# A written table in place of a build-time clock for the order of five engines' work

## The chip, the cores and the metric

The kernel runs on one core of one Trainium2 chip. The metric is the device time of one execution in microseconds (us). A core has five engines that each work through their own list of instructions in order and wait for one another by semaphores: TensorE (PE: matmuls, with weight loads, PEld, that overlap them), VectorE (DVE), ScalarE (ACT), GpSimd (POOL) and SyncE (SP), which here only starts transfers (DMAs). Matmuls write into PSUM, eight banks of 128 x 512 float32; everything else lies in SBUF, with 128 partitions.

## The reference

The input x has 2048 rows of 512 in bfloat16. Two attention layers and two feed-forward layers alternate, each on the layer norm of x and added to x, with the same weights both times:

```python
    x = A_x
    x = x + _A_ref(_layernorm(x, axis=-1), A_wq, A_wk, A_wv, A_wo, A_beta)
    x = x + _B_ref(_layernorm(x, axis=-1), B_w_gate, B_w_up, B_w_down)
    x = x + _A_ref(_layernorm(x, axis=-1), A_wq, A_wk, A_wv, A_wo, A_beta)
    x = x + _B_ref(_layernorm(x, axis=-1), B_w_gate, B_w_up, B_w_down)
```

`_B_ref` is `gelu(x @ w_gate) * (x @ w_up) @ w_down` with 1792 columns between. `_A_ref` is attention with a memory: 32 heads of 16, four segments of 512 rows that are worked through in order:

```python
            logits = jnp.einsum('bhqd,bhkd->bhqk', qs, ks) * scale + mask
            p = _softmax(logits, axis=-1)
            a_dot = jnp.einsum('bhqk,bhkd->bhqd', p, vs)
            pq = phi(qs)
            num = jnp.einsum('bhld,bhde->bhle', pq, M)
            den = jnp.einsum('bhld,bhd->bhl', pq, z)[..., None] + 1e-06
            a_mem = num / den
            o = g * a_mem + (1.0 - g) * a_dot
            outs.append(o)
            pk = phi(ks)
            M = M + jnp.einsum('bhld,bhle->bhde', pk, vs)
            z = z + jnp.einsum('bhld->bhd', pk)
```

Here `phi(t)` is t + 1 for positive t and exp(t) otherwise, and the mask leaves each query the keys up to its own place. The heads' results go through wo.

## The kernel before

x, all weights and one segment's intermediate results stay in SBUF. The work goes by segments of 512 rows: 8 for attention (4 in each of two layers) and 8 for the feed-forward layers, and work of neighbouring segments is mixed so that PE always has some.

**Attention, one segment.** Layer-norm statistics are taken on DVE; the normalised rows, xn, are written by DVE or POOL (L734), turned by a DMA or by PE (L425) into xnT, and multiplied with wq, wk and wv. Each product of 512 columns is four matmuls of 128 x 128 weights by 512 columns into a bank; the bank is copied ("evicted") by DVE (L601) or ACT (L602). kx holds two masked copies of k (L546, L551). Scores come in rounds: a visit of two rounds puts narrow matmuls of four row groups into four banks (`score`, L1670; "rows" mode: weights with 16 or 32 rows, four of them side by side in the array). ACT takes the exponential of a pair of banks at once (128 x 1024), or, where the four banks lie in a row, of all four (128 x 2048), into pt (L1710); POOL masks what lies on the diagonal (L1646, L1651), or DVE does (L1656). Value products multiply pt by the v of a segment (vaug, whose constant column gives the softmax sum, and vz for shared rounds) with four matmuls of 32 columns side by side ("columns" mode); DVE turns (L1209), scales (L1219) and turns back (L1232). phi is an exponential on ACT, a minimum with 1 on DVE or POOL (L989) and a max-and-add on DVE (L970). The memory's products give num and den, and its result is added to the heads' (L1235). Products with wo are added to x by DVE (L1287).

**Feed-forward, one segment.** 14 gate tiles (gelu on ACT), 14 up tiles (multiplied with the gate's on DVE, L1388), and 14 products to each of four blocks of rows by wd, added to x. wd_sb and gel_sb serve as buffers of the first segment until they are needed: rows of q and k of segment 0 lie in wd_sb.

**What sets the order.** `order` (L402) runs at build time. `Clocks` and four `Engine` objects hold a modelled time of each engine, with a cost per instruction. Work of the other engines is posted with a ready time and a slack, and each modelled engine takes the job with the least of them; evictions, masks, minima and xn may be posted to two engines, and whichever is free first by the model takes them. PE's work are items with a due time. The loop at the end of `order` asks at every step: are two score rounds ready and four banks free (`rounds_now`); is an item open; can one be opened in a free bank; and if nothing can, it issues a fill, a product of 128 columns on a tile of ones (`warm`), 24 times in all. Some 100 numbers in `POLICY`, with `CHANGES` per 20 us of modelled time, `NUDGES` and `VISITS`, weigh the choices. The model has a cost for changes of mode (`SWITCH`) and for instruction fetch (`sent`).

**Whole or columns.** The array takes a product as one matmul of 128 x 128 weights ("whole") or as four of 128 x 32 in columns mode, which is the mode of the value products. `product` (L605) decides by the mode PE is in, and by whether a value product is near:

```python
        if ck.mode == "columns" or ck.mode == "rows" and (any(it.kind == "flush" and it.near() for it in items)):
            ck.tiling("columns")
```

All of PE's matmuls go through `multiply` (L421).

Of the kernel before, what the change touches and what calls it, by code (L numbers as in the profile page):

```python
# [44 lines left out]
HALVED = ()  # L45
BOTH = (0, 1)
EARLY = [(1, 192, 64, 0), (0, 64, 192, 64)]
LATE = [([(3, 448, 64, 0), (2, 320, 192, 64)], 2), ([(0, 256, 256, 0)], 0), ([(1, 256, 256, 0)], 0)]


def shared(*tiles):
    return [(b, BOTH, ki, P * ki, C, C * n) for n, (b, ki) in enumerate(tiles)]


def whole_block(b):
    rounds = []
    for par in range(2):
        rounds += [([(b, (par,), *piece) for piece in pieces], n) for pieces, n in zip(FULL, DIAG)]
        if not par:
            rounds.append((shared(*((b, ki) for ki in range(TPS))), None))  # L60
    return rounds, ((0, 0, SHARED + 1), (1, SHARED, ROUNDS))


def table(halved):

    rounds, units = [], []

    def add(got):
        rounds.extend(got)
        return range(len(rounds) - len(got), len(rounds))  # L70

    def early(b):
        return [([(b, (par,), *piece) for piece in EARLY], 2) for par in range(2)]

    def late(b):
        return [([(b, (par,), *piece) for piece in pieces], n) for pieces, n in LATE for par in range(2)]

    for b in range(1 if halved else KT):
        got, parts = whole_block(b)
        at = add(got)  # L80
        units.append((b, None, [((par,), [at[i] for i in range(i0, i1)]) for par, i0, i1 in parts]))
    if halved:
        a1, s12, a2 = add(early(1)), add([(shared((1, 0), (1, 1), (2, 0), (2, 1)), None)]), add(early(2))
        a3, s3 = add(early(3)), add([(shared(*((3, ki) for ki in range(TPS))), None)])
        units += [(1, 0, [(BOTH, [*a1, *s12])]), (2, 0, [(BOTH, [*a2, *s12])]), (3, 0, [(BOTH, [*a3, *s3])])]
        units.append((3, 1, [(BOTH, [*s3, *add(late(3))])]))
        l1 = add(late(1))
        s12 = add([(shared((1, 2), (1, 3), (2, 2), (2, 3)), None)])
        units += [(1, 1, [(BOTH, [*l1, *s12])]), (2, 1, [(BOTH, [*s12, *add(late(2))])])]
    assert len(rounds) == STEPS  # L90
    flushes = [(u, b, h, n, pars, used) for u, (b, h, fl) in enumerate(units) for n, (pars, used) in enumerate(fl)]
    return rounds, len(units), flushes


TABLES = [table(k in HALVED) for k in range(NK)]
FLUSHES = [[[f for f in TABLES[k][2] if max(f[5]) == t] for t in range(STEPS)] for k in range(NK)]
USERS = [[sum(t in f[5] for f in TABLES[k][2]) for t in range(STEPS)] for k in range(NK)]
UNIT0 = [sum(TABLES[i][1] for i in range(k)) for k in range(NK)]
FLUSH0 = [sum(len(TABLES[i][2]) for i in range(k)) for k in range(NK)]


BY_PE = {("xnTf", 0), ("xnTf", 1), ("xnTf", NK - 1)}
QUICK = {("xnTf", k): (2,) for k in HALVED}
# [11 lines left out]
POLICY = dict(
    flush_wait=-12.009, piece_slack=-25.599, kb_slack=-71.296, mem_slack=-20.591, qk_due=-62.012, e_q=-288.808,
    e_k=138.109, exp_slack=-4.686, e_slack=148.266, phi_slack=52.68, gelu_slack=19.624, act_evict=2.071,
    first_evict=4.769, gate_step=1.835, up_due=3.98, up_step=-6.05, down_due=84.578, down_step=14.696, upd_due=9.144,  # L120
    kb_act=663.078, vz_slack=0.687, x_dve=-0.049, v0_due=-232.366, x1_at=-21.812, x2_at=-35.702, x3_at=1.468,
    x3_load=-242.902, direct=2, gelu_tiles=0, look=-61.488, lag=0, wv_at=-9.865, xn_pool=-26.108, kb_pool=62.128,
    cut_pool=0.028, at_pool=-27.695, gate_due=4.711, shun=77.466, col_gap=6.814, hold=34, early=435.185,
    starve=-5.581, near=-26.359, cap=6, soon=-134.054, drain=-0.14, join=0, held=10, urge_a1=-29.527, urge_a2=-0.64,
    urge_a3=-0.468, urge_a4=-5.519, urge_a5=-268.031, urge_a6=-6.935, urge_a7=-34.222, urge_f0=-37.767,
    urge_f1=-6.779, urge_f2=-11.706, urge_f3=-0.081, urge_f4=51.11, urge_f5=-14.712, urge_f6=-5.12, urge_f7=-38.117,
    half_a1=14, half_a4=21, half_a5=4, half_a6=18, half_a7=14, half_f0=21, half_f1=8, half_f2=10, half_f3=24,
    half_f4=46, half_f5=6, half_f6=8, pair_a1=10, pair_a2=3, pair_a3=12, pair_a4=11, pair_a5=0, pair_a6=65,
    pair_a7=28, pair_f0=9, pair_f1=19, pair_f2=43, pair_f3=2, pair_f4=22, pair_f5=23, pair_f6=28, pair_f7=11,
    turn_a1=14, turn_a2=12, turn_a3=8, turn_a4=8, turn_a5=6, turn_a6=16, turn_a7=42, turn_f2=18, turn_f3=4,  # L130
    turn_f4=16, turn_f5=2, turn_f6=6)

# [1723 lines left out]
```

## Time and profile before

| | |
|---|---|
| runs of the kernel, us | 539.11, 539.22, 541.04 (median 539.22) |
| span of the profiled execution, us | 539.1 |
| PE busy, us (instructions) | 521.3 (9,006 matmuls recorded) |
| weight loads, PEld | 274.5 (9,072) |
| DVE, ACT, POOL busy, us | 449.0, 433.2, 286.2 |
| bytes moved by DMA | 27.96 MB, mean 52 GB/s |

The profiled execution's own time is its span. Busy is time with at least one instruction under way; matmuls run in a pipeline, so their recorded durations overlap and the time from one start to the next is the price of one. A row of the groups gives line, engine, operation, out<-in, the shape, the count, then busy us, mean ns of one, and the idle time ahead of them with what ended it. A row of the windows gives a stretch, and busy us and instructions of PE, PEld, DVE, ACT and POOL in it, then PE's granted clock as a share of full speed, DMA share and GB/s. A row of the waits gives the waiting engine, tile and line, what it waited for, and total us, times and longest us. A row of the timeline gives start, duration, and in brackets the idle time ahead.

### The profile page before, as it was taken

Reading aid. Unit: us, or ns where it says so; the run is one execution under the profiler, and the core shown is the slowest. Engines: PE = TensorE matmul, PEld = TensorE weight load, DVE = VectorE, ACT = ScalarE, POOL = GpSimd, SP = SyncE. Lnnn points to the kernel's source line nnn. Section 1 sums busy time; section 2 is a strip of 40 time slices with the busy share of each in tenths; the row PEclk is TensorE's granted clock in tenths of the full one; section 3 lists DMA queues with packets and bytes.
Section 4 is the critical chain, followed back from the end, with each engine's and each line's share of the span. In section 5 each row is a group of like instructions: output and inputs, shape, how many; then the busy total and the mean of one; then the engine's idle time right before and its main releaser. Section 6 shows DMA issues by size and latency. Waiting matters only on the chain.

```text
span 539.1 us, 20839 instructions
## 1 busy us (share of the span) xinstructions
PE 521.3 (97%) x9006; PEld 274.5 (51%) x9072; DVE 449.0 (83%) x849; ACT 433.2 (80%) x559; POOL 286.2 (53%) x360
## 2 busy tenths in 40 slices
PE   8999999999999999999999999999989999999997
PEld 4444467446654454554544454454554456555444
DVE  7998897899999997898997999878988786786342
ACT  6999997998999978999899778889789968830320
POOL 4997853279778656647572387550655253301000
PEclk9999999999999999999999999999999999999999
DMA  8349302422011123311432120310121004100001
GB/s 270 85 109 208 93 19 54 128 41 62 13 32 41 24 46 49 52 33 21 52 80 32 23 43 12 71 35 9 33 71 24 0 16 98 14 2 30 11 0 40
DMA packets 69134, 27.96 MB, mean 52 GB/s; under 512 B 53426, under 2 KB 69042, under 8 KB 69042
## 3 DMA queue, kind: packets, MB, share of 16 engines
q1 hardware_dynamic: 68752, 26.36, 22.1%
q8 instruction: 71, 1.16, 0.9%
q10 hardware_dynamic: 290, 0.26, 0.1%
q14 instruction: 21, 0.17, 0.1%
HBM read 9.70 MB, written 2.10 MB: 22 GB/s over the span
## 4 chain that ended last, share of the span: by engine, by line
PE 77%; DVE 11%; DMA 4%; issue 3%; POOL 3%; ACT 2%; DVEq 0%; POOLq 0%; ACTq 0%
PE ps L421 76%; DVE st L684 2%; DVE x_sb L1287 2%; ACT pt L1710 2%; DVE xn L734 2%; DMA xnT<-xn 2%; DMA amT<-am 2%; DVE byq L1209 1%; DVE ab L1225 1%; POOL pt L1646 1%; PE ps L425 1%; DVE phiq L970 1%; POOL rs L721 0%; DMA x_sb<-in_A_x_dram 0%; POOL pt L1651 0%
## 5 line engine op out<-in xcount | busy, mean ns | idle before, releaser
L1710 ACT ACTIVATE pt<-ps 128x1024 bf16<-128x1024 f32 (+1 forms) x274 | 277.8, 1072 | 39.5 <-PE ps L421 34.4
L1646 POOL TENSOR_SCALAR_AFFINE_SELECT pt<-pt 128x256 bf16<-128x256 bf16 (+1 forms) x192 | 108.2, 577 | 143.1 <-ACT pt L1710 138.3
L421 PE MATMUL ps<-xnT,wg_sb 128*32 128x512 bf16 (+3 forms) x940 | 106.5, 362 | 1.4 <-issue 1.1
L421 PE MATMUL ps<-wd_sb,gel_sb 128*32 128x512 bf16 (+3 forms) x879 | 102.8, 364 | 2.9 <-issue 1.9
L421 PE MATMUL ps<-xnT,wu_sb 128*32 128x512 bf16 (+1 forms) x816 | 99.6, 379 | 0.6 <-issue 0.2
L1388 DVE TENSOR_TENSOR gel_sb<-gel_sb,ps 128x512 bf16<-128x512 bf16 x112 | 74.4, 682 | 23.6 <-PE ps L421 22.1
L421 PEld LDWEIGHTS <-gel_sb 128*32 128x32 bf16 (+1 forms) x1086 | 50.7, 97 | 45.1 <-issue 4.8
L421 PEld LDWEIGHTS <-wu_sb 128*32 128x32 bf16 (+1 forms) x826 | 44.4, 97 | 50.2 <-issue 0.6
L421 PEld LDWEIGHTS <-wg_sb 128*32 128x32 bf16 (+1 forms) x954 | 46.9, 97 | 38.3 <-issue 2.0
L1287 DVE TENSOR_TENSOR x_sb<-x_sb,ps 128x512 bf16<-128x512 bf16 (+1 forms) x68 | 43.1, 642 | 20.5 <-PE ps L421 20.2
L1209 DVE STREAM_TRANSPOSE byq<-ps 128x512 f32<-128x512 f32 x64 | 45.2, 709 | 14.6 <-PE ps L421 13.4
L989 POOL TENSOR_SCALAR e<-e 128x512 bf16<-128x512 bf16 x31 | 49.8, 1608 | 3.8 <-ACT e L966 3.1
L1651 POOL TENSOR_SCALAR_AFFINE_SELECT pt<-pt 64x1024 bf16<-64x1024 bf16 x34 | 39.4, 1158 | 14.7 <-ACT pt L1710 10.0
L1448 ACT ACTIVATE gel_sb<-gel_sb 128x512 bf16<-128x512 bf16 (+1 forms) x81 | 45.9, 652 | 0.1
L684 DVE BATCH_NORM_STATS2 st<-x_sb 128x6 f32<-128x512 bf16 x60 | 40.8, 679 | 0.3
L601 DVE CAST gel_sb<-ps 128x512 bf16<-128x512 f32 x48 | 32.3, 680 | 7.9 <-PE ps L421 7.4
L421 PE MATMUL ps<-pt,vaug 128*32 128x256 bf16 (+2 forms) x1344 | 35.4, 239 | 0.2 <-POOL pt L1646 0.2
L421 PE MATMUL ps<-xnT,wk_sb 128*32 128x512 bf16 (+3 forms) x238 | 33.8, 353 | 0.5 <-issue 0.3
L421 PE MATMUL ps<-xnT,wq_sb 128*128 128x512 bf16 (+3 forms) x205 | 32.3, 347 | 2.0 <-DMA xnT<-xn 0.9
L421 PEld LDWEIGHTS <-vaug 128*32 128x32 bf16 x1344 | 26.7, 97 | 11.6 <-issue 4.2
L421 PE MATMUL ps<-q,kx 32*128 32x64 bf16 (+2 forms) x1120 | 30.8, 217 | 0.8 <-DVE x_sb L1287 0.8
L421 PE MATMUL ps<-wv_sb,xnT 128*32 128x512 bf16 (+1 forms) x194 | 30.6, 380 | 1.1 <-issue 0.6
(116 smaller groups left out, 704.4 us busy)
## 6 DMA issues: line engine op xcount, KB each, us to landing
vz<-vaug SPq DMA_DIRECT2D x14, 136.0 KB, 2.9
wg_sb<-in_B_w_gate_dram SPq DMA_DIRECT2D x8, 224.0 KB, 4.0
wu_sb<-in_B_w_up_dram SPq DMA_DIRECT2D x8, 224.0 KB, 4.4
wd_sb<-in_B_w_down_dram SPq DMA_DIRECT2D x7, 256.0 KB, 3.5
x_sb<-in_A_x_dram SPq DMA_DIRECT2D x3, 512.0 KB, 6.6
out_dram<-x_sb SPq DMA_DIRECT2D x12, 128.0 KB, 1.8
xnT<-xn SPq DMA_TRANSPOSE x48, 2.4
wk_sb<-in_A_wk_dram SPq DMA_DIRECT2D x2, 256.0 KB, 4.2
```

The source lines that it names most:

```text
L421: nc.tensor.matmul(*args, **named)
L601: ck.dve.post(ck.made(), slack + pol.drain, (0.673, lambda: nc.vector.tensor_copy(out=dst(), in_=src()), end), taken=taken)
L684: nc.vector.bn_stats(out=self.st6[:, 0, :], in_=x_sb[:, self.tt0 + j, :])
L734: eng.tensor_scalar(out=xn[:], in0=x_sb[:, self.tt0 + j, :], scalar1=self.mv[:, j, 1:2] if self.quick else self.mv[:, j, 0:1], scalar2=sel ...
L989: lambda eng: eng.tensor_scalar(out=e[0][:], in0=e[0][:], scalar1=1.0, scalar2=None, op0=ALU.min), summed)
L1209: nc.vector.transpose(out=(self.byq[:, pars[0], :, :].rearrange("p a c -> p (a c)") if h is None else self.byq[:].rearrange("p u a c -> p ...
L1287: ck.dve.post(ck.made(), slack, (0.15 + 0.00104 * (c1 - c0), lambda: nc.vector.tensor_tensor(out=xt, in0=xt, in1=ps()[:, 0:c1 - c0], op=AL ...
L1388: ck.dve.post(ck.made(), pol.drain, (0.683, lambda: nc.vector.tensor_tensor(out=g, in0=g, in1=ps()[:], op=ALU.mult), lambda t: (ps.read(t) ...
L1448: return (0.205 + 0.427 * (f1 - f0), lambda: nc.scalar.activation(out=g, in_=g, func=ACT.Gelu_apprx_tanh), lambda t: self.gelu_done(t, f0, ...
L1646: nc.gpsimd.affine_select(out=view, in_=view, pattern=[[0, 4], [0, n], [1, C]], compare_op=ALU.is_ge, fill=0.0, base=C, channel_multiplier=-1)
L1651: nc.gpsimd.affine_select(out=view, in_=view, pattern=[[0, 4 * TPS], [1, C]], compare_op=ALU.is_ge, fill=0.0, base=0, channel_multiplier=-1)
L1710: nc.scalar.activation(out=pt_all[:, slots[0]:slots[0] + 2, 2 * p:2 * p + 2 * n, :].rearrange("p r h c -> p h r c"), in_=ps_all[:, b0:b0 + ...
```

## The change

`Clocks`, `Engine`, `Item`, the policy numbers and all code that chooses go. In their place stands `ORDER`, a string of some 2,700 tokens, and `run`, which goes through it once and issues what each token names. A token is a code and numbers: `S/0/1/3/5/2` is the score visit 1 of segment 0 in the banks from 3 and from 5, into pt slot 2; `E/0/0` takes its exponential over four banks, `e/k/v/p` over the pair p; `Q/0/1/0/1/1/0` is one matmul step (the fifth field) of wq's product 1 of segment 0 in bank 1, whole (a last field of 1 means columns); `q/v/0/1` evicts it by DVE (`v`), ACT (`s`); `M/g/0/0` masks a round by POOL (`g`) or DVE. So order, bank, buffer, engine and mode are all given by the table. There are no fills. What is computed stays the same.

Counted over the two built programs: matmuls 9,072 before, 10,508 after (as many weight loads); products of 512 columns 1,716 in both, of which in columns 481 before, 837 after; of 256 columns 432 in both, in columns 165 and 277; changes of PE's mode 319 and 291; PE's tile turns 64 and 48 matmuls, and turns by DMA 48 and 52; exponentials over two banks 260 and 182, over four 14 and 53; xn on DVE 57 and 40, on POOL 7 and 24; half masks on POOL 34 and 20, the masks on DVE in their place 15 and 22; minima on DVE 17 and 25, on POOL 31 and 23.

```diff
-POLICY = dict(
-    flush_wait=-12.009, piece_slack=-25.599, kb_slack=-71.296, mem_slack=-20.591, qk_due=-62.012, e_q=-288.808,
...
-class Clocks:
...
+ORDER = """
+S/0/0/4/6/0 c/0 Q/0/1/0/1/1/0 E/0/0 K/0/1/0/1/2/0 m/v/0/0 Q/0/1/0/1/1/0 K/0/1/0/1/2/0 Q/0/1/0/2/1/0 st/1/0 q/v/0/1
...
-    def product(out, lhsT, rhs, start=True, stop=True):
-
-        if ck.mode == "columns" or ck.mode == "rows" and (any(it.kind == "flush" and it.near() for it in items)):
-            ck.tiling("columns")
+    def product(dst, lhsT, rhs, columns, start=True, stop=True):
+        if columns:
             for c in range(4):
                 r = slice(32 * c, 32 * c + 32)
-                multiply(out[r], lhsT=lhsT[:, r], rhs=rhs, start=start, stop=stop, tile_position=(0, 32 * c))
-            ck.count += 4
+                multiply(dst[r], lhsT=lhsT[:, r], rhs=rhs, start=start, stop=stop, tile_position=(0, 32 * c))
         else:
-            ck.tiling("whole")
-            ck.count += 1
-            multiply(out, lhsT=lhsT, rhs=rhs, start=start, stop=stop)
+            multiply(dst, lhsT=lhsT, rhs=rhs, start=start, stop=stop)
...
+    for token in ORDER:
+        code, *arg = token.split("/")
...
+        if code in ("Q", "K", "V", "O", "G", "P", "QH", "KH", "GH", "W"):
+            dense(code, *i)
+        elif code == "S":
+            score(*i)
+        elif code == "F":
+            values(*i)
...
-            if streams:
-                ps = Psum()
-                ps.bank = bank
-                product(ps()[:, 0:P], warm[:], wide[:, 0, :])
```

Two places show what the table moves. The first is DVE's list in segments 0 and 1, some 50 us into the run. In the list before, row 98 is the 106th instruction, the eviction of a v tile; kx are the masked key copies, e the exponential of phi, phiq its result for q.

```order
94 L546 TENSOR_SCALAR kx_120<-kf,masks 128x4x64
95 L546 TENSOR_SCALAR kx_120<-kf,masks 128x4x128
96 L546 TENSOR_SCALAR kx_120<-kf,masks 128x4x64
97 L546 TENSOR_SCALAR kx_120<-kf,masks 128x4x128
98 L601 CAST vaug_138<-ps 128x16x2x16
99 L970 SCALAR_TENSOR_TENSOR phiq<-q,e 128x512 x2
```

At the like point of PE's work the list of DVE in the changed kernel is at row 112, the 118th instruction, an eviction of q:

```order
105 L861 TENSOR_SCALAR e<-e 128x512 x2
106 L680 SCALAR_TENSOR_TENSOR e,zk<-wd_sb,e 128x512
107 L509 CAST q<-ps 128x512
108 L509 CAST vaug_134<-ps 128x16x2x16
109 L680 SCALAR_TENSOR_TENSOR phiq<-q,e 128x512
110 L509 CAST vaug_134<-ps 128x16x2x16
111 L861 TENSOR_SCALAR e<-e 128x512
112 L509 CAST q<-ps 128x512
```

More evictions, minima and phi sums stand ahead of it, and by the whole list up to there fewer xn. The second place is PE's list ahead of the 42nd value product (segment 5, in the second attention layer, mixed with a feed-forward segment): products of gel_sb with wd_sb, and then the value product (`pt`, `vaug`). Before, each product is one matmul:

```order
11125 L421 LDWEIGHTS gel_sb
11126 L421 MATMUL ps<-wd_sb,gel_sb 128x512
11127 L421 LDWEIGHTS gel_sb
11128 L421 MATMUL ps<-wd_sb,gel_sb 128x512
11129 L421 LDWEIGHTS gel_sb
11130 L421 MATMUL ps<-wd_sb,gel_sb 128x512
11131 L421 LDWEIGHTS gel_sb
11132 L421 MATMUL ps<-wd_sb,gel_sb 128x512
11133 L421 LDWEIGHTS vaug_138
11134 L421 MATMUL ps<-pt,vaug_138 32x256
```

In the changed kernel a product is four matmuls of 32 columns, the mode that the value product needs:

```order
12529 L498 LDWEIGHTS gel_sb
12530 L498 MATMUL ps<-wd_sb,gel_sb 32x512
12531 L498 LDWEIGHTS gel_sb
12532 L498 MATMUL ps<-wd_sb,gel_sb 32x512
12533 L498 LDWEIGHTS gel_sb
12534 L498 MATMUL ps<-wd_sb,gel_sb 32x512
12535 L498 LDWEIGHTS gel_sb
12536 L498 MATMUL ps<-wd_sb,gel_sb 32x512
12537 L648 LDWEIGHTS vaug_134
12538 L648 MATMUL ps<-pt,vaug_134 32x256
```

The change of mode has moved from just ahead of the value product to an earlier place, and PE's list has more instructions for the same product.

More of the change, by code (lines that the diff above doesn't have):

```diff
@@ L1 @@
-import heapq
 from contextlib import ExitStack
@@ L59, in whole_block @@
         if not par:
[L60 to L103, printed above, removed]
+            rounds.append(([(b, BOTH, ki, P * ki, C, C * ki) for ki in range(TPS)], None))
+    return rounds
+ROUNDS_OF = [r for b in range(KT) for r in rounds_of(b)]
+USED = [(0, SHARED + 1), (SHARED, ROUNDS)]
 BANKS = 8
@@ L1463, in order, with tile_of @@
[L1463 to L1479 removed]
+    def tile_of(m):
+        return TPS * (m % NSEG)
@@ L1481, in first_stats @@
+    xnT[0] = place(seg, [P, KT, L], "xnTa0", "xnT")
+    q[0], kf[0] = (wd_sb[:, KT * i:KT * (i + 1), :] for i in range(2))
+    kx[0] = kx0
+    st6 = [place(wrk, [P, 1, 6], "bnst", "st6", F32, 4) for _ in range(TPS - 1)]
     def first_stats(j):
```

1900 lines of the change are left out of this document (640 added, 1260 removed).

## Prediction

> **What bounds the kernel now.** I read the page's head and its chain first, then a table of windows, the waits of TensorE (PE), and the timeline where PE waits.
>
> ```profile
> span 539.1 us, 20839 instructions
> PE 521.3 (97%) x9006; PEld 274.5 (51%) x9072; DVE 449.0 (83%) x849; ACT 433.2 (80%) x559; POOL 286.2 (53%) x360
> PE 77%; DVE 11%; DMA 4%; issue 3%; POOL 3%; ACT 2%; DVEq 0%; POOLq 0%; ACTq 0%
> ```
>
> PE is busy 97% and carries 77% of the chain: over the whole span no other engine can be the bound. That is an average, so the stretches come next.
>
> ```profile
> core 0: us, PE busy (x) PEld busy (x) DVE busy (x) ACT busy (x) POOL busy (x), PEclk, DMA share, GB/s
> 0.00:10.00 10.00, 7.81 (x45) 4.02 (x45) 6.57 (x23) 4.85 (x11) 3.62 (x15) 1.00 0.81 249
> 0.00:49.60 49.60, 45.73 (x590) 22.10 (x598) 43.32 (x108) 43.83 (x65) 40.02 (x57) 1.00 0.63 162
> 49.60:105.00 55.40, 53.42 (x1001) 32.35 (x1006) 48.83 (x91) 50.88 (x69) 29.67 (x39) 1.00 0.31 86
> 105.00:175.00 70.00, 69.00 (x1248) 38.38 (x1258) 67.05 (x128) 66.34 (x89) 55.41 (x61) 1.00 0.18 39
> 175.00:360.00 185.00, 180.78 (x3518) 91.86 (x3543) 166.32 (x318) 161.90 (x203) 109.70 (x133) 1.00 0.23 40
> 360.00:450.00 90.00, 86.79 (x1556) 44.55 (x1561) 75.33 (x127) 76.69 (x90) 39.78 (x56) 1.00 0.14 31
> 450.00:540.00 90.00, 85.53 (x1121) 45.29 (x1118) 48.16 (x82) 33.55 (x47) 11.66 (x17) 1.00 0.10 24
> ```
>
> The granted clock is 1.00 throughout. From 10 to 49.6 us VectorE (DVE) works 43.32 − 6.57 = 36.75 of 39.6 us, so it idles only 2.85; from 105 to 175 us only 2.95. In these two stretches PE leads, but DVE follows with no slack to speak of.
>
> ```profile
> PE ps L421 <- issue: 6.8, 37, 1.1
> PE ps L421 <- DVE warm L464: 1.1, 1, 1.1
> PE ps L421 <- DMA xnT<-xn: 1.1, 3, 0.6
> PE ps L421 <- DVE byq L1209: 1.0, 2, 0.8
> PE ps L421 <- DVE x_sb L1287: 0.8, 1, 0.8
> ...
> 535.99 0.42 DVE x_sb L1287
> ```
>
> Each row gives the total, the number and the longest wait: all are small. The last row is the last sum after PE's last product; from there to the end are 3.1 us of adding and storing that the change leaves alone.
>
> **The change, part by part.** The sum is made against the profiled execution's 539.1 us, 0.1 under the median of 539.22.
>
> *PE's own work.* First the price of one product, whole or in columns:
>
> ```profile
> 262.80 0.82 PE L421 MATMUL ps<-wd_sb,gel_sb 128*128 128x512 bf16 x3
> 263.46 0.55 PE L421 MATMUL ps<-zcols,phiq 128*128 128x8 bf16 x16
> ...
> 186.22 0.28 PE L421 MATMUL ps<-q,kf 16*128 16x256 bf16 x4
> 186.43 0.83 PE L421 MATMUL ps<-wo_sb,aT 128*32 128x512 bf16 x12
> ...
> 187.64 1.25 PE L421 MATMUL ps<-wd_sb,gel_sb 128*32 128x512 bf16 x20
> 188.83 0.40 PE L421 MATMUL ps<-q,kf 16*128 16x64 bf16 x12
> ```
>
> Three whole products take 0.66 us from start to start, 0.22 each. Five in columns (20 matmuls) take 1.19 us with one change of mode. One pass of four 256-wide score matmuls and a change take 0.21; a 256-wide pass being half of a 0.216 us product, the change costs 0.10, and the five products (1.19 − 0.10)/5 = 0.22 each. So the mode costs nothing by itself. Counted in the order of both kernels, 356 products of 512 columns go from whole to columns (whole 1,235 to 879; total 1,716 in both): no time. Changes of mode fall from 319 to 291, 28 × 0.10 = 2.8 us saved.
>
> ```profile
> L421 PE MATMUL ps<-warm 128*128 128x128 bf16 x19 | 2.4, 220 | 0.3 <-ACT wd_sb L602 0.2
> ```
>
> The fills (these 19 and five in columns) and 16 of the 64 tile turns go: 40 products of 128 columns at a quarter of 0.216, 2.2 us. They ran where PE had nothing else, so the fills' share is real only if PE has work in their places. Together **−5.0 us**.
>
> ```profile
> L421 PEld LDWEIGHTS <-wu_sb 128*128 128x128 bf16 x322 | 31.1, 98 | 37.3 <-issue 0.4
> L421 PEld LDWEIGHTS <-wu_sb 128*32 128x32 bf16 x504 | 13.3, 97 | 12.9 <-issue 0.2
> ```
>
> A weight load takes 98 ns for 128 columns and 97 for 32, so four cost 290 ns more than one; 356 times that would be 103 us if it showed, and the pitches above show none of it. The Trainium skill (TensorEngine Tiling (Array Packing), Gotcha 2: Feature Incompatibilities) says that column tiling gives up the fast weight load, which speaks against this change; the 97 ns are for a quarter of the columns, as such a rule would have it, but the load lies under the running matmul.
>
> *DVE ahead of PE at 50 us.* This is the term against the change.
>
> ```profile
> 48.70 0.68 DVE L601 CAST vaug<-ps 128x512 bf16<-128x512 f32 x1
> 49.30 1.28 DVE L970 SCALAR_TENSOR_TENSOR phiq<-q,e 128x512 bf16<-128x512 bf16 x2
> ...
> 49.61 0.40 PE L421 MATMUL ps<-wd_sb 16*128 16x64 bf16 x12
> ```
>
> Before, the scores at 49.61 need DVE's 106th instruction, the eviction that ends at 49.38. At that point PE has issued 141 products of 512 columns. At the like point of the table (151 products) PE needs DVE's 118th, an eviction of q. What lies ahead of it on DVE differs:
>
> ```profile
> L601 DVE CAST kf<-ps 128x512 bf16<-128x512 f32 x16 | 10.9, 680 | 4.5 <-PE ps L421 4.4
> L970 DVE SCALAR_TENSOR_TENSOR phiq<-q,e 128x512 bf16<-128x512 bf16 x24 | 16.9, 714 | 0.1
> L970 DVE SCALAR_TENSOR_TENSOR e<-kf,e 128x512 bf16<-128x512 bf16 x20 | 15.2, 762 | 0.4 <-POOL e L989 0.3
> L989 DVE TENSOR_SCALAR e<-e 128x512 bf16<-128x512 bf16 x17 | 6.5, 390 | 0.6 <-ACT e L966 0.4
> L1656 DVE TENSOR_TENSOR pt<-pt,tri 128x1024 bf16<-128x1024 bf16 x15 | 13.6, 910 | 0.7 <-ACT pt L1710 0.7
> L734 DVE TENSOR_SCALAR xn<-x_sb,mv,rs 128x512 bf16<-128x512 bf16 x57 | 28.7, 540 | 2.6 <-POOL rs L721 1.6 <-DMA phik<-e 0.5 <-DMA amT<-am 0.3
> ```
>
> Seven more evictions (8 to 15 counting all), 7 × 0.680 = 4.76; five more phi sums, 2 × 0.714 + 3 × 0.762 = 3.71; five more minima, 1.95; one more mask, 0.91; four fewer xn, −2.16. The masked key copies cancel. That is 9.2 us, less 12 overlaps of consecutive instructions (0.08 in the rows above: 49.30 against 49.38), some 0.7: 8.5 us. PE's own list up to there grows only by ten products less some fills and changes, 1.9 us. So PE could be there at 49.6 + 1.9 = 51.5, and DVE at 49.38 + 8.5 = 57.9 if it idles as much as before, or at 55.0 if all of its 2.85 us of idleness after 10 us goes. PE comes 3.5 to 6.4 us late; I take the middle, **+5.0 us**.
>
> *What is late next.* After that point PE idles by the windows 1.98 + 1.00 + 4.22 + 3.21 + 0.4 = 10.8 us; 66 records are missing there or earlier, and counted by pitches it loses 9.3 us (1.6 of them to instruction fetch, below). The other 7.7 are many short waits, none over 1.0, on engines that have little more to do after that point. DVE's whole list grows by some 9 to 10 us (ten evictions, eight minima, seven masks and four sums more, 17 xn fewer), 8.5 of it ahead of that point; ACT's falls:
>
> ```profile
> L1710 ACT ACTIVATE pt<-ps 128x1024 bf16<-128x1024 f32 x260 | 251.6, 1029 | 34.5 <-PE ps L421 29.7 <-POOL pt L1646 3.3 <-issue 0.5
> L1710 ACT ACTIVATE pt<-ps 128x2048 bf16<-128x2048 f32 x14 | 26.2, 1875 | 5.0 <-PE ps L421 4.7 <-issue 0.2
> ```
>
> Exponentials over four banks rise from 14 to 53 and pairs fall from 260 to 182: 39 × (2 × 1.029 − 1.875) = 7.1 us less on ScalarE (ACT). A PE that is 5 us later finds such results made. Those that go round through PE itself (scores, exponential, mask, values) don't gain by its lateness, so I count three quarters as gone: **−5.8 us** (bounds 0 and −7.7). Where PE catches up again, the cover is gone; this is rival A. GpSimd (POOL) takes 17 more xn and gives up 14 half masks and others, +0.8 us net at 53% load; SP gets four more turning DMAs, and the evictions moved between DVE and ACT sit in their queues ahead of masks and phi: all nothing while PE is late.
>
> *Instruction fetch.*
>
> ```profile
> q8 instruction: 71, 1.16, 0.9%
> ...
> 85.45 0.28 PE L421 MATMUL ps<-pt,vz 128*32 128x64 bf16 x13
> 86.79 0.21 PE L421 MATMUL ps<-pt,vz 128*32 128x64 bf16 x3 [1.06 <-issue]
> ```
>
> 71 packets of 16 KB answer to PE's 18,144 loads and matmuls (256 to a packet). One gap of 1.06 us stands inside a value product, waiting for no engine. It falls 184 instructions past a multiple of 256, where 290 instructions from 150 to 440 past one need only 2.32 us by pitches; the shortfall to 3.4 us is 1.08, like the gap. Four such stretches of before are under 3.4 (2.32, 3.11, 3.29, 3.30; 1.6 us short), and five of the new order's 82 blocks (1.92, 2.35, 2.65, 3.06, 3.09; 3.9 us short): **+2.3 us**, an estimate on one row. The Trainium skill (Runtime: NRT & Kernel Launch, Instruction fetch mechanics) agrees on the 16 KiB blocks and holds the fetch for hidden behind issue; by that this term is 0 and the time 533.4, but the gap speaks against it.
>
> Sum: 539.1 − 5.0 + 5.0 − 5.8 + 2.3 = 535.6; with the 0.1 to the median, **535.7 us**.
>
> **The rivals.** *A: DVE stays the bound to 175 us.* The new order has some 9 us more DVE work ahead of PE up to there by the same count; DVE idled 2.85 + 6.57 + 2.95 us after the first 10. If the stretch 105 to 175 cannot absorb it, PE is late there again by 3 to 5 us: 535.7 + 4 = 539.7, no change. For it: 96% busy in that stretch, and waits planned with under 0.5 us to spare, 84 against 34. Against it: 6.6 us of idleness from 49.6 to 105. Chance 0.27.
>
> *B: DVE's idleness closes up.* At 50 us PE is 3.5 late, all the 7.7 go, fetch as forecast: 539.1 − 5.0 + 3.5 − 7.7 + 2.3 = 532.2; without the fetch term 529.9. Chance 0.15.
>
> *C, slower: fetch.* Each column product issues eight instructions in the time of two, and the new order needs 11 blocks more. If each of these costs the 1.06 us of the gap, the time is 535.7 − 2.3 + 11.7 = 545.1; it decides from eight gaps on (541.9). Against it: 71 blocks made one gap of note. Chance 0.11.
>
> *D: the order changes nothing that PE feels.* The same products at 97% busy, fewer changes eaten by what waits they uncover: 539. Chance 0.08.
>
> **How the numbers follow.** The forecast (533 to 536.5) has the rest, 0.39. Half a per cent, 2.7 us, is about what a measurement of this kernel can tell from no change: same is 536.5 to 541.9. Faster is forecast and B, 0.54; same A and D, 0.35; slower C, 0.11. The range 530.0 to 541.5 leaves out C and the ends of A and B. The forecast's own is 533 to 536.5.
>
> **What would show it.** Right: PE's granted clock 1.00, its waits named DVE between 45 and 60 us adding up to 3.5 to 6.4, and less than 4 us of engine waits after them; DVE over 95% busy from 10 to 57 us; 82 instruction packets, with gaps of about 1 us inside value products. Wrong: no PE wait on DVE near 50 us (then B), waits on DVE from 105 to 175 us (A), ten or more gaps "issue" of 1 us (C), or a pitch of products in columns above 0.22 (then the 356 cost).

## The result and the profile after

The changed kernel takes 546.16 us (four runs, 546.02 to 546.25), the kernel before 539.61 on the same chip: ratio 1.0119, interval 1.0104 to 1.0133. It is slower by 6.6 us; the forecast was 535.7, and the range ended at 541.5.

In nearly every run the time lies 1.7 to 1.9 us above the span (546.14 at a span of 544.3). The prediction took them for one. By that, the profiled execution of before (span 539.1) was one of its slower ones: eleven later runs have spans from 536.4 to 539.2, median 537.6. The two errors nearly cancel in the level, but the profiled loss of before is 1.5 us more than usual. Between the two profiled spans the change costs 5.3 us, between the times 6.6. The one profile of e16 (below) was taken at a granted clock of 0.75 and is not used.

The windows after, in the same cuts from 49.6 us on (stretch, then busy us and instructions of PE, PEld, DVE, ACT, POOL, clock, DMA share, GB/s):

```profile
0.00:10.00 10.00, 8.37 (x45) 4.11 (x45) 6.36 (x20) 4.85 (x11) 3.66 (x15) 1.00 0.84 254
10.00:49.60 39.60, 33.75 (x546) 16.14 (x545) 34.62 (x86) 33.16 (x42) 31.87 (x37) 0.96 0.47 106
49.60:105.00 55.40, 53.60 (x1263) 32.86 (x1264) 49.95 (x94) 51.36 (x59) 33.28 (x42) 1.00 0.41 106
105.00:175.00 70.00, 68.71 (x1562) 39.70 (x1554) 65.65 (x125) 64.73 (x78) 45.48 (x57) 1.00 0.30 46
175.00:360.00 185.00, 183.43 (x3526) 92.47 (x3525) 166.08 (x321) 157.29 (x185) 113.29 (x134) 1.00 0.23 38
```

From 10 to 49.6 us PE is busy for 33.75 us, where before it was 45.73 − 7.81 = 37.92, and the clock is no longer 1.00. The waits of PE say where, and the timeline of PE shows what follows:

```profile
PE ps L498 <- DMA xnT<-xn: 4.5, 1, 4.5
PE ps L610 <- ACT pt L615: 2.5, 5, 0.9
PE ps L358 <- DVE warm L350: 1.1, 1, 1.1
PE ps L498 <- issue: 1.0, 2, 0.6
```

```profile
21.57 0.40 PE L610 MATMUL ps<-wd_sb 32*128 32x64 bf16 x12 [0.30 <-ACT pt L615]
26.47 0.89 PE L498 MATMUL ps<-wv_sb,xnT 128*32 128x512 bf16 x8 [4.50 <-DMA xnT<-xn]
27.13 0.66 PE L498 MATMUL ps<-xnT,wq_sb 128*32 128x512 bf16 x4
27.55 0.66 PE L498 MATMUL ps<-xnT,wk_sb 128*32 128x512 bf16 x4
```

One wait of 4.5 us, for the turned x of segment 1; before, no wait for xnT was over 0.6. Behind it six products start 0.42 us apart, twice their usual distance: 1.3 us more, with the granted clock at 0.55 in that stretch (shown at e2). After that PE is late but hardly waits any more. From 28 to 62 us it has one wait, and none for DVE:

```profile
PE ps L610 <- ACT pt L615: 0.5, 1, 0.5
```

DVE is busy for 41.88 of the 47 us from 10 to 57 us, which is 89%. POOL and SP show where xnT was held:

```profile
18.24 2.10 POOL L408 TENSOR_SCALAR xn<-x_sb,mv,rs 128x512 bf16<-128x512 bf16 x1
20.28 0.49 POOL L625 TENSOR_SCALAR_AFFINE_SELECT pt<-pt 128x256 bf16<-128x256 bf16 x1
20.77 2.07 POOL L408 TENSOR_SCALAR xn<-x_sb,mv,rs 128x512 bf16<-128x512 bf16 x1
```

```profile
17.58 1.29 SPq L883 DMA_TRANSPOSE xnT<-xn  x1
19.80 1.36 SPq L329 DMA_DIRECT2D vz<-gel_sb  x2
21.25 9.07 SPq L883 DMA_TRANSPOSE xnT<-xn  x5
```

The table gives two of the four xn to POOL, at 2.1 us each, and puts the two vz loads between the turns on SP, which wait for an eviction. The tile that PE needs first is turned last. Before, DVE made the four xn and SP issued the four turns in a row from 17.10.

For what follows I count PE's *lost time*: the start of a matmul in the trace less the pitches (times from one start to the next without a wait) and changes of mode of all matmuls ahead of it in the list. The pitches and changes are PE's *own work*. The count uses the prices of the prediction and the whole list, so that missing records don't disturb it.

| PE's own work ahead, us | 14 | 26 | 42 | 62 | 122 | end |
|---|---|---|---|---|---|---|
| lost before, us | 4.7 | 6.0 | 6.3 | 6.7 | 9.4 | 15.6 |
| lost after, us | 5.5 | 12.2 | 13.3 | 14.6 | 19.4 | 26.1 |

Own work to the end is 520.1 before and 515.1 after, and 2.9 instead of 3.1 us follow. So −5.0, +7.0 lost by the 42nd us of own work, +3.5 lost afterwards and −0.2 make the 5.3 us between the two spans. Of the 7.0, 5.4 arise between the 14th and the 26th us of own work, where the wait for xnT stands; of the 3.5, 3.0 arise between the 42nd and the 122nd.

### The profile page after: what moved, and what is told of

It reads as the page before. It is cut to its first block, busy times and chain, and to the rows that moved or that the text cites. A ratio compares the mean times of both kernels' runs of the same rounds, so it can differ in the third digit from the quotient of the medians.

```text
span 544.3 us, 23608 instructions
## 1 busy us (share of the span) xinstructions
PE 527.6 (97%) x10508; PEld 281.9 (52%) x10508; DVE 447.9 (82%) x861; ACT 423.9 (78%) x509; POOL 284.7 (52%) x357
## 4 chain that ended last, share of the span: by engine, by line
PE 80%; DVE 7%; POOL 3%; DMA 3%; ACT 3%; issue 3%; SPq 0%; ACTq 0%; DVEq 0%; POOLq 0%
PE ps L498 34%; PE ps L500 32%; PE ps L610 7%; PE ps L648 5%; ACT pt L615 3%; DMA xnT<-xn 1%; POOL xn L408 1%; DVE byq L655 1%; DMA wo_sb<-in_A_wo_dram 1%; DVE x_sb L774 1%; POOL pt L625 1%; DVE am L730 1%; DMA amT<-am 1%; POOL rs L520 1%; DMA x_sb<-in_A_x_dram 1%
## 5 line engine op out<-in xcount | busy, mean ns | idle before, releaser
L836 DVE TENSOR_TENSOR gel_sb<-gel_sb,ps 128x512 bf16<-128x512 bf16 x112 | 72.7, 682 | 23.0 <-PE ps L498 15.6
L498 PE MATMUL ps<-wd_sb,gel_sb 128*32 128x512 bf16 (+1 forms) x1168 | 62.3, 356 | 0.8 <-ACT pt L615 0.8
L498 PE MATMUL ps<-xnT,wg_sb 128*32 128x512 bf16 (+1 forms) x1004 | 61.3, 359 | 0.9 <-issue 0.6
L500 PE MATMUL ps<-xnT,wg_sb 128*128 128x512 bf16 (+1 forms) x253 | 56.7, 354 | 0.8 <-DVE am L730 0.8
L498 PE MATMUL ps<-xnT,wu_sb 128*32 128x512 bf16 x892 | 55.9, 379 | 0.0
L408 POOL TENSOR_SCALAR xn<-x_sb,mv,rs 128x512 bf16<-128x512 bf16 x24 | 52.2, 2176 | 2.4 <-DVE q L509 1.2
L500 PE MATMUL ps<-xnT,wu_sb 128*128 128x512 bf16 x225 | 52.6, 379 | 0.2 <-DVE byq L655 0.2
L500 PE MATMUL ps<-wd_sb,gel_sb 128*128 128x512 bf16 (+1 forms) x212 | 46.3, 356 | 0.1
L770 ACT ACTIVATE gel_sb<-gel_sb 128x512 bf16<-128x512 bf16 x82 | 44.4, 622 | 0.0
L498 PEld LDWEIGHTS <-gel_sb 128*32 128x32 bf16 x1168 | 30.1, 97 | 23.0 <-issue 1.1
L500 PEld LDWEIGHTS <-wu_sb 128*128 128x128 bf16 x225 | 21.6, 98 | 26.3 <-issue 1.1
L498 PEld LDWEIGHTS <-wg_sb 128*32 128x32 bf16 x1004 | 24.9, 96 | 19.4 <-issue 3.1
```

What stands on the lines that cost most here:

```text
L408: eng.tensor_scalar(out=xn[:], in0=x_sb[:, tile_of(m) + j, :], scalar1=mv[:, m, j, 0:1], scalar2=rs[:, m, j, :], op0=ALU.subtract, op1=ALU ...
L498: multiply(dst[r], lhsT=lhsT[:, r], rhs=rhs, start=start, stop=stop, tile_position=(0, 32 * c))
L500: multiply(dst, lhsT=lhsT, rhs=rhs, start=start, stop=stop)
L770: nc.scalar.activation(out=dst, in_=src, func=ACT.Gelu_apprx_tanh)
L836: nc.vector.tensor_tensor(out=gel_sb[:, b, :], in0=gel_sb[:, b, :], in1=ps("P", k, b, 0), op=ALU.mult)
```

## Experiments

Each kernel was timed in five rounds against the kernel before, whose medians beside them lie between 539.19 and 539.73.

| | us | | us |
|---|---|---|---|
| changed kernel | 546.16 | e10 before, 128 later | 542.80 |
| e1 xn early | 544.95 | e11 after, 64 later | 545.44 |
| e2 fill in the wait | 542.63 | e12 after, 128 later | 549.14 |
| e3 all whole | 553.57 | e13 DVE's order | 548.47 |
| e4 vz late | 544.87 | e14 e13, less on DVE | 548.36 |
| e5 e1 and e8 | 547.91 | e15 PE later at 69 us | 553.68 |
| e6 fill, 152 later | 547.92 | e16 e1, some on POOL | 548.58 |
| e7 e5, statistics later | 547.65 | e17 after, 36 later | 544.63 |
| e8 seven evictions on ACT | 548.73 | e18 e1, short statistics | 543.12 |
| e9 before, 64 later | 542.86 | | |

### The wait at 22 us: e1, e4, e2

e1, the four xn on DVE, their turns ahead of vz:

```diff
-... sc/1/1 xn/v/1/1/2 ... xt/1/1 ... xn/g/1/2/3 ... z/0 ... xn/v/1/3/4 ... xn/g/1/0/5 ... xt/1/2 ... xt/1/3 ... xt/1/0
+... sc/1/1 xn/v/1/1/2 xn/v/1/2/3 xn/v/1/3/4 xn/v/1/0/5 ... xt/1/1 xt/1/2 xt/1/3 xt/1/0 ... z/0
```

> The changed kernel with the four xn of segment 1 all on DVE, right after their scales, and their turning DMAs ahead of the two vz loads on SP; nothing else moved. Theory 1 (the 4.5 us wait of PE for xnT at 22 us, and the six passes at 0.427 us behind it, 1.3 us, are the loss): the wait falls to 0.5 to 2 us and the time to 541 to 542. Theory 2 (DVE has 8.5 us more ahead of PE's 151st product, so PE is held there whatever happens at 22 us): the wait at 22 us goes, PE waits for DVE from 30 to 60 us instead, and the time falls by less than 2, to 544 or more.

544.95 us (ratio to before 1.0105, 1.0084 to 1.0126), 1.2 less than the changed kernel: nearer to theory 2. The median mixes two kinds of run: in three of the six the mean granted clock was 1.000 (543.80 to 544.30 us), in three 0.996 or 0.997 (545.60 to 547.06). At full clock e1 is thus 2.1 us faster than the changed kernel. In the profiled execution the wait fell from 4.5 to 1.65 us and the clock stayed at 1.00, but in PE's timeline a new wait begins 5 us on:

```profile
24.20 0.62 PE L498 MATMUL ps<-wv_sb,xnT 128*32 128x512 bf16 x8 [1.65 <-DMA xnT<-xn]
...
31.45 0.29 PE L648 MATMUL ps<-pt,gel_sb 128*32 128x256 bf16 x4 [2.26 <-DVE byq L655]
```

DVE's timeline shows that it was never idle ahead of that turn (byq, 30.69): statistics, constants and xn of segments 2 and 3 stand there.

```profile
28.65 0.44 DVE L757 COPY vaug<-cden 128x128 bf16<-128x128 bf16 x1
28.77 0.43 DVE L408 TENSOR_SCALAR xn<-x_sb,mv,rs 128x512 bf16<-128x512 bf16 x1
...
30.08 0.68 DVE L680 SCALAR_TENSOR_TENSOR e<-wd_sb,e 128x512 bf16<-128x512 bf16 x1
30.69 0.08 DVE L680 DVE_READ_ACCUMULATOR e<-wd_sb,e 128x1 f32 x1
30.69 0.71 DVE L655 STREAM_TRANSPOSE byq<-ps 128x512 f32<-128x512 f32 x1
```

e4, only the vz loads moved:

```diff
-... E/0/3 z/0 ... xt/1/0 M/g/0/4
+... E/0/3 ... xt/1/0 z/0 M/g/0/4
```

> The changed kernel with the two vz loads moved behind the four turning DMAs of segment 1 on SP; xn as in the changed kernel. The last turn can then be issued when POOL's xn is done (22.84 us) instead of 23.9: the wait at 22 us shrinks by 1.0 us, and the time by 1 if that wait is on the path, by 2.3 if PE's idleness falls under what makes the next passes slow, by nothing if DVE holds PE later.

544.87 us, 1.3 less; the wait is 3.5 instead of 4.5, as expected, and the slow passes stayed.

e2, 18 products on the tile of ones ahead of the waiting one:

```diff
-V/1/0/0/2/7/1
+fill/18/7 V/1/0/0/2/7/1
```

> The changed kernel with 18 products on the tile of ones put where PE waits for xnT at 22 us (3.9 us of work that fills the wait, outputs not used). If the slow passes behind the wait (0.427 us each) come of PE's idleness, they run at 0.216 and the time falls by 1.2 to 1.3 us, to 544.9; if PE would be held by DVE afterwards anyway, the time stays at 546.2 within 0.5.

542.63 us, 3.5 less, more than expected (e17 takes the rest up). The windows, first the changed kernel, then e2, show the granted clock (last but two) behind the wait:

```profile
26.40:29.20 2.80, 2.73 (x28) 1.15 (x32) 1.89 (x9) 0.60 (x1) 2.58 (x5) 0.55 0.06 12
```

```profile
26.40:29.20 2.80, 2.80 (x88) 1.66 (x84) 1.93 (x8) 1.23 (x2) 2.63 (x6) 1.00 0.62 50
```

0.55 against 1.00, and 28 against 88 matmuls. That the slow passes come of PE's idleness is shown. The Trainium skill (TensorE: Matmul & The Clock Gate, What's actually happening) has the array at half clock after about 3.4 us without work; 4.5 us here agree. The clock also fell behind shorter waits, of 3.1 us in e13 and of 2.2 us in e5 (both below), so 3.4 us is not a safe limit for this kernel.

### What limits PE from 22 to 58 us: e8, e5, e7, e13, e14, e16, e18

e8 is the changed kernel and e5 is e1 with seven evictions on ACT:

```diff
-q/v/0/2 ... q/v/1/1 ... q/v/1/0 ... q/v/1/3 ... v/v/1/1 ... v/v/1/2 ... k/v/1/3
+q/s/0/2 ... q/s/1/1 ... q/s/1/0 ... q/s/1/3 ... v/s/1/1 ... v/s/1/2 ... k/s/1/3
```

> The changed kernel with only those seven evictions moved to ACT; xn as in the changed kernel, so the xnT wait at 22 us stays. If the two are two limits side by side (PE is late by xnT at 22 us, and by DVE's list at 58 us, and the later of them decides), this alone gives 1.5 us or less, 544.6 to 546, and e5 gives more than this and e1 together. If they add up, it gives 3 to 4.5.

> The kernel of e1 with seven evictions of segments 0 to 1 (four of q, two of v, one of k, all ahead of PE's 151st product) taken by ACT instead of DVE, each at its place in the table. If DVE's list holds PE as soon as the xnT wait is gone: 7 x 0.68 = 4.8 us of DVE work fewer, PE 3 to 4.5 us earlier at 58 us, time 540.5 to 542. If the loss behind 30 us is of another kind (PE's own order, ACT, POOL): within 1 us of e1, 544 to 546.

548.73 and 547.91 us: 2.6 and 3.0 slower than without the move. Neither theory had that. PE now waits for ACT, whose evictions stand behind exponentials in its list (PE's timeline in e8):

```profile
34.59 0.81 PE L500 MATMUL ps<-xnT,wq_sb 128*128 128x512 bf16 x2 [0.88 <-ACT q L507]
...
42.49 0.63 PE L648 MATMUL ps<-pt,gel_sb 128*32 128x256 bf16 x24 [0.57 <-ACT vaug L507]
```

In the changed kernel ACT idles 6.4 of the 39.6 us from 10 to 49.6, but not at these places. e5 is not a clean test of the move, because in its profiled execution the granted clock is 0.57 from 30 to 38 us, behind a wait that left the clock at 1.00 in e1's:

```profile
31.16 0.40 PE L648 MATMUL ps<-pt,gel_sb 128*32 128x256 bf16 x4 [2.20 <-DVE byq L655]
...
35.10 1.91 PE L500 MATMUL ps<-xnT,wk_sb 128*128 128x512 bf16 x4
```

The next row starts at 36.80, so four products take 1.70 us, twice the usual. Aligned instruction by instruction, e5's PE is 2.4 us behind e1's at 40 us and 3.9 at 50. The last 1.5 us are what e8 also loses between 40 and 50 us. All four runs of e5 have a mean clock below 1.000.

e7 is e5 with the statistics of segment 3 (`st/3`) moved behind the turns. e13 (shown) is the same without ACT, with two constants (`c/2`, `c/3`) moved too, and with the turn that PE needs first issued first:

```diff
-... F/0/0/3 ... f/0/0 ... F/0/1/3 ... xn/g/3/1/3 ... f/0/1
+... F/0/0/3 v/s/1/0 f/0/0 c/2 ... F/0/1/3 ... c/3 st/3/0 st/3/1 st/3/2 st/3/3 sc/3/2 xn/g/3/1/3 ... f/0/1
```

> The kernel of e5 with the four statistics of segment 3 (4 x 0.84 us on DVE) moved behind the first two turns of the value products. In e1 PE waited 2.3 us at 29 us for such a turn, behind statistics, constants and xn on DVE. If DVE's order there is a limit of its own, 1 to 2 us faster than e5; if only the sum of DVE's work ahead of 58 us counts, within 0.7 of e5.

> The changed kernel with DVE's list put in another order, nothing taken from it but two xn of POOL's that it gets: the four xn of segment 1 first (their turns ahead of vz on SP), the four statistics of segment 3 and two constant columns behind the first turns of value products. Both waits seen so far (4.5 us for xnT in the changed kernel, 2.3 us for the turn in e1) are then out of PE's way. If the order of DVE's list at 17 to 31 us is the loss: PE 3 to 4 us earlier at 58 us, 541.5 to 543. If DVE's sum ahead of 58 us is the limit, as the prediction had it: it ends at most 1.5 us earlier, 544 to 546.

547.65, within noise of e5, and 548.47, slower than e1 and than the changed kernel: neither expectation of e13 held. In e13 both old waits are short, and PE waits for the second turn, behind the statistics that were moved there:

```profile
35.02 0.58 PE L500 MATMUL ps<-wv_sb,xnT 128*128 128x512 bf16 x1 [3.14 <-DVE byq L655]
35.41 1.91 PE L500 MATMUL ps<-xnT,wk_sb 128*128 128x512 bf16 x4
37.11 1.91 PE L500 MATMUL ps<-xnT,wq_sb 128*128 128x512 bf16 x4
```

The next products are slow again (35.41 to 37.11 for four, 0.43 each from start to start). e14 is e13 with six minima and a mask left out:

```diff
-n/v/1/0/1 ... n/v/1/0/2 ... n/v/0/1/2 ... n/v/1/0/3 ... n/v/0/1/3 ... n/v/0/1/0 ... M/v/0/13
```

> The kernel of e13 with some of DVE's work ahead of 60 us left out: six minima with 1 (phi comes out larger for large arguments) and one mask of a half diagonal, 6 x 0.39 + 0.91 = 3.3 us; outputs are not the reference's. If DVE's sum is the limit: 2 to 3 us faster than e13. If not: within 0.7 of e13.

548.36: no difference, but it says little, since all of that work except one minimum stands behind the wait at 31 us. In e16 POOL takes over three constants, a minimum and a masked pair:

```diff
-n/v/1/0/1 ... m/v/0/2
+n/g/1/0/1 ... m/g/0/2
...
+        eng = nc.gpsimd if 0 < n < 4 else nc.vector
```

> The kernel of e1 with three constant columns, one minimum and one pair of masked key copies, all ahead of the first turn of the value products on DVE, done by POOL, which has little to do from 18 to 32 us there: 3 x 0.48 + 0.28 + 0.62 = 2.3 us off DVE's list, the order of the rest untouched. If DVE's sum ahead of that turn holds PE: the 2.3 us wait at 29 us goes, and the time falls by 1.5 to 2.5 from e1's 544.95, to 542.5 to 543.5. If not (or if POOL's slower copies hold ACT or PE): 544 to 546.

548.58: slower. In POOL's list the masked pair and a constant now stand ahead of a mask that the first value product needs; whether that holds PE no undisturbed profile shows. e18 takes work off DVE without lengthening another queue:

```diff
-        nc.vector.bn_stats(out=st[:, 0, :], in_=x_sb[:, tile_of(m) + j, :])
+        w = 32 if m in (2, 3) else D
+        nc.vector.bn_stats(out=st[:, 0, :], in_=x_sb[:, tile_of(m) + j, 0:w])
```

> The kernel of e1 with the statistics of segments 2 and 3 taken over 32 columns of 512 (so their layer norm is not the reference's): eight instructions of 0.68 us on DVE become short, some 4 us less ahead of the first turn, and no queue's order changes. If DVE's sum ahead of that turn holds PE at 29 us: the waits there (2.4 and 0.6 us in e1) go, and the time falls by 2 to 3 from e1's 544.95, to 542 to 543. If something else holds PE there too: 544 to 546.

543.12 (ratio 1.0063, 1.0048 to 1.0078), 1.8 less than e1 and just above the range expected. All six runs have the clock at 1.000; against the three such runs of e1 (median 544.08) the gain is 1.0, and the rest is the clock. The wait for the turn is 0.36 us instead of 2.26 (PE's timeline):

```profile
29.59 0.29 PE L649 MATMUL ps<-pt,gel_sb 128*32 128x256 bf16 x4 [0.36 <-DVE byq L656]
```

So DVE's sum ahead of that turn holds PE there, once xnT is in time. Up to that turn DVE is busy for 23.4 us in the changed kernel and for 21.6 before (one more eviction, two constants, a phi sum, a minimum, a masked pair; one xn fewer). The xnT wait stands in front of this limit, and so taking it away in e1 gave 1.2 us (2.1 at full clock) and not the 5.8 of the wait and the slow passes.

### Does lateness cover later waits? e15

```diff
-O/0/0/0/1/4/0
+fill/12/4 tiny/116/4 O/0/0/0/1/4/0
```

> The changed kernel with 128 products on the tile of ones at 68.8 us (12 of 512 columns, 116 of 8; 5.6 us of PE's time by pitches, 256 instructions, one whole block, so that the phase of what follows stays). If a PE that is late finds results made and waits less afterwards, as the prediction had it: the 11.5 us that it loses after that point fall by 2 to 4, and the time rises by 1.5 to 3.5 only. If lateness covers nothing, because the other engines' work hangs on PE's: the time rises by 5 to 6, to 551 to 552.

553.68 us, 7.5 slower, more than the 5.6 put in. The profiled execution is 6.6 us longer than that of the changed kernel. Aligned instruction by instruction it is 1.0 us behind already ahead of the fill, with the clock at half from 25.4 to 32.2 us and not only from 26.7 to 30.1; it is 6.3 behind after the fill and 6.6 at the end. So 5.6 us put in cost 5.6: a PE that is late waits as much, and its lateness covered nothing. This was tried at one place.

### Whole and columns: e3

```diff
-        if columns:
+        if False:
```

> The changed kernel with every dense product and memory product whole, order otherwise untouched: 837 products of 512 columns and 277 of 256 go back from four matmuls to one, changes of mode rise from 291 to 405. If columns cost nothing by themselves: 114 x 0.10 = 11.3 us slower, 557.5, less a microsecond or two for instruction fetch (57 blocks instead of 82). If column products or their instructions are the loss, the time rises by less than 6 or falls.

553.57, 7.4 slower instead of 11.3: between the two expectations. Own work is 11.3 more (526.4), lost time falls from 26.1 to 21.9. With 56 instruction packets instead of 82, e3 has no stretch short of 3.4 us by the rule of the prediction, where the changed kernel has 3.9 us of shortfall; but PE also leaves other engines 11 us more, and the instructions stand otherwise against the blocks of 256. The 114 changes of mode cost more than the columns do; what makes up the 3.9 us between 11.3 and 7.4 stays open.

### The phase of the instruction blocks: e6, e17, e9 to e12

The *phase* is how the list of PE's instructions lies against the blocks of 256 that one instruction packet brings.

```diff
-V/1/0/0/2/7/1
+fill/12/7 tiny/64/7 V/1/0/0/2/7/1
```

> The changed kernel with 76 products on the tile of ones in PE's wait at 22 us, 12 of 512 columns and 64 of 8 (4.3 us together, nearly as much as e2's 18), so that all that follows stands 152 instructions later against the blocks of 256. By the rule of the prediction (the stretch from 150 to 440 past a block's start takes at least 3.4 us) the shortfalls of the changed kernel are 3.9 us, of e2 2.9, of this one 0.7: 2.2 us faster than e2, 540.4. If instruction fetch costs nothing, or its gaps don't follow the count, as e2: 542.6.

547.92, 5.3 more than e2, whose PE list differs only in the fill. The rule of the prediction had promised 2.2 less: as a forecast of the time it falls. One place of the loss is at 101 us, where DVE, not PE, waits for a turning DMA; DVE's timeline in e6, then the same add in e2:

```profile
103.78 0.42 DVE L777 TENSOR_TENSOR aT<-aT,amT 128x512 bf16<-128x512 bf16 x1 [1.83 <-DMA amT<-am]
```

```profile
102.52 0.43 DVE L777 TENSOR_TENSOR aT<-aT,amT 128x512 bf16<-128x512 bf16 x1 [0.62 <-DMA amT<-am]
```

The DMA rows of these stretches (packets by queue, then issues with the median us to landing), e6 from 100.5 to 103.7 and e2 from 99 to 103:

```profile
q1 hardware_dynamic: 1136, 0.30, 84.7%
q8 instruction: 1, 0.02, 1.9%
...
amT<-am SPq DMA_TRANSPOSE x2, 3.6
```

```profile
q1 hardware_dynamic: 1369, 0.51, 65.5%
q14 instruction: 1, 0.01, 0.6%
...
amT<-am SPq DMA_TRANSPOSE x2, 2.5
```

In e6 an instruction packet of PE (q8, from 101.9 to 102.9 us) falls on the turn (100.7 to 104.3), which then takes 3.6 us, not 2.5; the gelu products behind that add on DVE come 1.3 us later, and PE waits 1.5 us for one. That is 1.3 of the 5.3 us between the two profiled spans. Another 1.4 stand behind the last sum, in the last store; the rest was not traced.

e17, e11 and e12 shift the changed kernel by 36, 64 and 128 instructions, e9 and e10 the kernel before by 64 and 128, with the order untouched (w warming products and t of 8 columns in place of 12; the edit shown is that of the changed kernel):

```diff
-    for _ in range(WARM):
+    for _ in range(w):
...
+    for _ in range(t):
+        multiply(ps_all[:, 0, 0:8], lhsT=warm[:], rhs=warm[:, 0:8], start=True, stop=True)
```

> The changed kernel 36 instructions later (8 warming products and 22 of 8 columns in place of 12), nothing put into the wait at 22 us: the phase of e2 without its fill. e2 was 3.5 us faster than the changed kernel, of which the six slow passes are 1.3. If the other 2.2 are the phase: 544.0. If they belong to the fill: 546.2.

> The kernel before with 6 of its 12 warming products at the start replaced by 38 of 8 columns, which take about as long there: the order of all five engines' work stays, but all that follows stands 64 instructions later against the blocks of 256 in which PE's instructions are fetched. Theory phase (a fetch that falls on a turning DMA makes it land 3.6 to 4.1 us after its issue, not 2.4, in the profiles so far, and the block's phase decides which are hit): the time moves by 1 to 5 us, up or down; up if the order before was fitted to its own phase. By the starvation rule of the prediction alone (1.58 against 0.16 us of shortfall): 1.4 faster. If fetch costs nothing: 539.4 within 0.7.

> The same with 3 warming products and 73 of 8 columns, 128 instructions later. Theory phase: moves by 1 to 5 us. Starvation rule alone (1.98 against 1.58): 0.4 slower. If fetch costs nothing: 539.4 within 0.7.

> The changed kernel with the same 6 warming products and 38 of 8 columns: order and the wait at 22 us untouched, 64 instructions later. Theory phase: moves by 1 to 5 us from 546.2, and the mean over phases 0, 64 and 128 says how much of the 6.8 between the two kernels belongs to the order and how much to the phase it was compared at. Starvation rule alone (3.93 against 1.52): 2.4 faster, 543.8.

> The changed kernel 128 instructions later, with 3 warming products and 73 of 8 columns. Theory phase: moves by 1 to 5 us from 546.2. Starvation rule alone (3.93 against 1.62): 2.3 faster, 543.9. If fetch costs nothing: 546.2 within 0.7.

Before: 539.19, 542.86, 542.80 us at 0, 64 and 128; after: 546.16, 544.63, 545.44, 549.14 at 0, 36, 64 and 128. The single runs of e9 spread widely, from 540.62 to 545.09.

These moves are not the phase alone. The shortened warming makes the start slower: the same products in e10, then in the kernel before:

```profile
9.35 1.92 PE L421 MATMUL ps<-xnT,wq_sb 128*128 128x256 bf16 x8
```

```profile
8.55 1.04 PE L421 MATMUL ps<-xnT,wq_sb 128*128 128x256 bf16 x8
```

By 13 us the profiled executions are late by 1.4 us (e9, e12, e17), 1.5 (e11) and 1.7 (e10), and they stay so until 20 us at least. With that taken off, the phase moved the time by about −3.0 us (e17), −2.2 (e11), +1.6 (e12), +2.2 (e9) and +1.9 (e10). e17 and e12, with one order and one start, lie 4.5 us apart, so the phase is real.

Of e2's 3.5 us, 1.3 are the slow passes; the phase of e17, some 3.0, is more than the 2.2 that are left, but within the intervals. The rule of the prediction (the shortfalls) had foretold −1.4, +0.4, −2.4 and −2.3 for e9 to e12: it comes near for e11 alone. The mean over 0, 64 and 128 is 541.6 before and 546.9 after, with nearly the same loss at the start in both: 5.3 of the difference belongs to the order, and about 1.3 to the phase at which the kernel before stands, its best of the three. Three phases are a small sample.

## Why the prediction was wrong

**What bounds it: right, and not enough.** PE is busy 97% after as before. I looked for the next limit at one place, 49 us, where DVE ended 0.23 us ahead of PE, and not at what the new SP and POOL lists put ahead of PE's first use of each tile.

**PE's own work, −5.0: stands.** Products in columns start 0.22 us apart as counted, and own work is 5.0 less. What was saved was lost again in waits.

**POOL and SP put at nothing: the step that failed first.** "SP gets four more turning DMAs, and the evictions moved between DVE and ACT sit in their queues ahead of masks and phi: all nothing while PE is late". The prediction also counted the xn moved to POOL by POOL's load (53%) and not by the 2.1 us that each takes on the way to PE. In its place the trace shows 4.5 us of waiting for xnT at 22 us and 1.3 us of slow passes, at a point where PE was only 0.8 us later than before (lost time 5.5 against 4.7).

**DVE ahead of PE, +5.0: near the 7.0 measured, but by luck.** PE was 7.0 us late by the 42nd us of own work (bounds 3.5 to 6.4), and DVE's 118th instruction, forecast to end at 57.9, ended at 58.58:

```profile
57.90 0.68 DVE L509 CAST q<-ps 128x512 bf16<-128x512 f32 x1
```

But the mechanism is not the one of the prediction. PE's trace has no wait for DVE from 28 to 62 us but for a product at 58.64 that starts 0.2 us late behind this row, where 3.5 to 6.4 us were to show, and DVE was busy 89% from 10 to 57 us, not over 95. From 10 to 58.6 us DVE idled 5.1 us, 3.7 of them waiting for PE: the two are late together, behind xnT. DVE's list is the next limit, at 31 us and not at 50; that shows only where xnT is in time (e1, e18). The sum itself has a slip: twelve overlaps of 0.08 are 1.0 us, not 0.7.

**What is late next, −5.8: the step that failed most.** Lost time after that point rose by 3.5. The forecast for it, with the 2.3 of the fetch, was −3.5. That is 7.0 of the 8.7 us between the forecast sum (535.6) and the span (544.3); the rest is 2.0 of the term on DVE (7.0 for 5.0), less 0.2 behind PE's last product, within rounding. Lateness covered nothing where it was tried (e15). That the reason is that each engine's list hangs on PE's scores and products is argued, not shown.

**Instruction fetch, +2.3: seen, but smaller.** Two of the three gaps stand 184 instructions past a block's start, as forecast, the third 180 (the longest: 0.59 us at 88.78, waiting for "issue"). They come to 1.4 us, against the one of 1.06 before: 0.3 more, not 2.3. Rival C, a gap for each of the added blocks, did not happen. What was missed is that a packet also goes with slower turning DMAs. The Trainium skill (Runtime: NRT & Kernel Launch, Instruction fetch mechanics) has the fetch mostly hidden; the phases above, 4.5 us apart for one order of work, speak against it for this kernel.

**Rivals.** A named DVE as the lasting limit and gave 539.7; PE was late and never caught up, but its sign failed: PE's waits for DVE from 105 to 175 us come to 0.2 us. The sign of B, no wait for DVE near 50 us, came without its time (532.2). The slower case was given 0.11, for another mechanism.

Open: what the 3.5 us after 58 us are made of (packets on turning DMAs, and the table's narrower planned leads, are candidates), and how much a table with one early xnT and a shorter DVE list would win. No kernel here beats the one before.

## What to carry to other kernels

When an order is written out, check each queue by itself at PE's first use of every tile: the sum of what stands ahead, slow engines and DMA issues included, not the engine's load. Don't credit lateness with covering later waits: here it covered nothing (e15). Look at the clock of every run before a median is read: e1's 1.2 us were 2.1 at full clock. And compare two orders at several phases of the instruction blocks before a difference of under 1% is put down to the order, with a shift that leaves the start alone.

## What the runs showed of the hardware

A turning DMA takes 2.44 us from issue to landing without an instruction packet of PE under way (median of 45 in the changed kernel), 3.63 with one (43); before, 2.34 (46) and 4.12 (26). A packet counts if it runs later than 1 us after the issue. In all profiles used the two medians lie 1.1 to 1.8 us apart. That the packet delays the turn was seen at the place looked at (e6), not forced.

Shifting all instructions by 36 to 128 moved the time by −1.5 to +3.7 us with no change in any engine's order; with the 1.4 to 1.7 us of the shortened warming taken off, by −3.0 to +2.2.

In every profile used a wait of PE of 3.1 us (e13) or more goes with passes at half speed, six of them in the changed kernel (1.3 us). Below that it can go either way: half speed with 2.2 us in e5, none with 2.26 in e1 and 2.4 in e7, and e1's own six runs divide three to three.

An xn of 128x512 takes 2.18 us on POOL and 0.51 on DVE (means of 24 and 40 in the changed kernel).
